# One gate-and-up product of a fused attention/SwiGLU kernel, run as two 64-row halves of TensorE

## The chip, the cores and the metric

The kernel runs on one core of a Trainium2 chip. The metric is the device time of one execution in microseconds, lower is better. Profiles are of one execution each; "span" is the time from its first to its last instruction.

## The reference

Input `x` has 2048 rows of 1024 values in bf16. `xn` is its layernorm. One branch is a local dilated attention (32 heads of 32 values, a window of 8 positions 2 apart), the other a SwiGLU MLP of inner width 3584; the result joins them:

```python
x = A_x
xn = _layernorm(x, axis=-1)
s = _A_ref(xn, A_wqkv, A_wo)              # qkv product, windowed softmax attention, product with wo
g = _silu(_B_ref(xn, B_w1, B_w3, B_w2))   # _B_ref: (silu(xn @ w1) * (xn @ w3)) @ w2
return x + s * g
```

## The kernel before

The 2048 rows are worked off in four chunks of 512 (`for c in range(NCH)`, line 592). In each chunk TensorE does, in this order:

- `qkv` (line 274): 24 groups of 8 matmuls; a group adds up the 1024 values of the contraction in 8 steps (`kt`) of 128 rows, into one PSUM tile of 128 x 512 float32. ScalarE copies each out (line 272).
- the MLP's first product, `up_block` (line 254), for 14 blocks (`FB`) of 256 columns of w1 and w3. A block has two slices of 128 columns; for each, a gate group (w1) and an up group (w3) of 8 matmuls, through `mm_group` (line 243). That makes 56 groups or 448 matmuls in a chunk. `gate_up` (line 247) follows each pair of groups: ScalarE applies silu to the gate's PSUM tile, VectorE multiplies that with the up group's PSUM tile and writes `ht`.
- the second product in two halves of the output columns (`down_half`, line 454 for its matmuls), with the attention's product with wo (line 409) in the midst of the second half.

Groups take their PSUM tiles from one pool of six (`psum_mm`). Weights come in tiles of 512 KB through SyncE's DMA queue into a pool of nine (`NS`); `take_w` hands out the next, and `load_w` issues the load of a later one once a tile has been used.

The attention's vector work, the next chunk's layernorm and the output's last steps lie in a list, `Side`. After each group or pair the program calls `side.step`, which emits as many entries as the time of that group covers, by costs written next to each entry; an entry may have a gate, an earliest time on that list's own clock. So VectorE's and ScalarE's instruction order is fixed by where these calls stand among TensorE's groups. During the first product of a chunk the list holds the query-key products (lines 299 to 314), the next chunk's statistics (line 190), its square root on ScalarE (line 216), the softmax (lines 352 to 364) with its Exp on ScalarE (line 346), and the product of probabilities and values (lines 383 and 394), which waits for a shuffle of the probabilities by DMA (`Pr<-pb`, line 372). Every engine executes its instructions in the order of the program.

Of the kernel before, what the change touches and what calls it, by code (L numbers as in the profile page):

```python
# [8 lines left out]
FP32 = mybir.dt.float32  # L9
# [36 lines left out]
def kernel(  # L46
# [11 lines left out]
    nc = tc.nc  # L58
    P = 128
    S, D, F = 2048, 1024, 3584  # L60
    Dh, W, DIL = 32, 8, 2
    KT = D // P
    CH = 512
# [3 lines left out]
    FB = FT // 2  # L67
# [4 lines left out]
    GRP = 1.727  # L72
# [13 lines left out]
    psum_mm = ctx.enter_context(tc.tile_pool(name="psum_mm", bufs=6, space=bass.MemoryType.PSUM))  # L86
# [13 lines left out]
    side = Side()  # L100

    def block(name):
        return blk.tile([P, 4096], BF16, tag="blk", name=name)
# [13 lines left out]
    def load_w(n=1, cuts=1):  # L117
        for _ in range(n):
            item = next(w_next, None)
            if item is None:  # L120
                return
            wt = wstream.tile([P, 2048], BF16, tag="w", name="w" + item[0])
            if item[0] == "q":
                _, t, a = item
                view = wt.rearrange("p (k c) -> p k c", k=2)
                src = wqkv_r[:, 2 * a:2 * a + 2, t * D:(t + 1) * D]
            elif item[0] == "2":
                _, dh, fb = item
                view = wt.rearrange("p (i n) -> p i n", n=512)
                src = w2_r[:, fb * 4:(fb + 1) * 4, dh * 512:(dh + 1) * 512]  # L130
            else:
                view = wt.rearrange("p (k f) -> p k f", k=KT)
                src = (w1_r if item[0] == "1" else w3_r)[:, :, item[1] * 256:(item[1] + 1) * 256]
            step = view.shape[1] // cuts
            for i in range(cuts):
                nc.sync.dma_start(out=view[:, i * step:(i + 1) * step, :], in_=src[:, i * step:(i + 1) * step, :])
            w_tiles.append((item, view))

    def take_w(item):
        got, wt = w_tiles.popleft()  # L140
        assert got == item, (got, item)
        return wt
# [9 lines left out]
    for st in range(1, NST):  # L152
# [7 lines left out]
    scr = const.tile([P, 1], FP32, name="scr")  # L160
# [4 lines left out]
        out=ident[:], in_=ident[:], compare_op=ALU.not_equal, fill=1.0,  # L165
# [5 lines left out]
        out=maskb[:], in_=maskb[:], compare_op=ALU.is_ge, fill=-1.0e9,  # L171
# [8 lines left out]
    def load_wo():  # L180
        was = []
        for dh in range(2):
            wa = block("wo").rearrange("p (j n) -> p j n", n=CH)
            nc.sync.dma_start(out=wa, in_=wo_r[:, :, dh * 512:(dh + 1) * 512])
            was.append(wa)
        return was
# [51 lines left out]
    def bring_one():  # L238
        if brings and brings[0][0] <= side.now:
            brings.popleft()[1]()  # L240


    def mm_group(ps, lhs, rhs):
        for kt in range(KT):
            nc.tensor.matmul(ps, lhsT=lhs(kt), rhs=rhs(kt), start=(kt == 0), stop=(kt == KT - 1))  # L245

    def gate_up(g_ps, u_ps):
        sg = sgp.tile([P, CH], BF16, tag="sg")
        nc.scalar.activation(out=sg[:], in_=g_ps[:], func=ACTF.Silu)  # L249
        ht = hp.tile([P, CH], BF16, tag="ht")  # L250
        nc.vector.tensor_mul(ht[:], sg[:], u_ps[:])  # L251
        return ht

    def up_block(c, xnT, fb):
        hts = []
        w1t, w3t = take_w(("1", fb)), take_w(("3", fb))
        for i in range(2):
            pss = []
            for wt in (w1t, w3t):
                ps = psum_mm.tile([P, CH], FP32, tag="mm", name=f"gu{c}_{fb}_{len(pss)}")  # L260
                mm_group(ps[:], lambda kt: wt[:, kt, i * P:(i + 1) * P], lambda kt: xnT[:, kt, :])
                pss.append(ps)
            if i == 1:
                load_w(2)
            hts.append(gate_up(*pss))
            side.step(2 * GRP, 0.7)
        bring_one()
        return hts
# [5 lines left out]
    def qkv(c, xnT, ts):  # L274
        for t in ts:
            w = take_q(t)
            if t == 1 and c > 0:
                nc.gpsimd.tensor_copy(out=kT[:, :, 0:HALO], in_=kT[:, :, CH:CH + HALO])
            if t == 2 and c > 0:
                nc.gpsimd.tensor_copy(out=vT[:, :, 0:HALO], in_=vT[:, :, CH:CH + HALO])  # L280
            for j in range(NJ):
                ps = psum_mm.tile([P, CH], FP32, tag="mm", name="ps_qkv")
                mm_group(ps[:], lambda kt: w(kt, j), lambda kt: xnT[:, kt, :])
                if j == NJ - 1:
                    load_w(4)
                proj_out(t, j, ps)
                side.step(GRP)
            if t == 1:
                qk_side(c)
# [125 lines left out]
    def wo_proj(pieces, was):  # L415
        side.flush()
        oT = att["oT"]
        s_sb = block("s_sb").rearrange("p (st d) -> p st d", st=NST)
        for dh, st in pieces:
            ps = wo_piece(oT, was, st, dh * CH, CH)  # L420
            nc.scalar.copy(out=s_sb[:, st, dh * CH:(dh + 1) * CH], in_=ps[:])  # L421
            side.step(GRP)
        return s_sb
# [14 lines left out]
    def finish_half(c, dh, gts, s_sb, xres, queue):  # L438
        def one(st):
            finish(c, st, dh * 512, 512, gts[st][:], s_sb[:, st, dh * 512:(dh + 1) * 512], xres, queue)  # L440
        for st in range(NST):
            side.add(1.38, lambda st=st: one(st))

    def down_half(c, dh, hts, at):
        accs = [psum_mm.tile([P, 512], FP32, tag="mm", name=f"acc{c}_{dh}_{st}") for st in range(NST)]
        gts = []
        for fb in range(7):
            w2t = take_w(("2", dh, fb))
            order = [(i, st) for i in range(4) for st in range(NST)]
            if fb in (0, 6):  # L450
                order = [(i, st) for st in range(NST) for i in range(4)]
            for n, (i, st) in enumerate(order):
                f = fb * 4 + i
                nc.tensor.matmul(  # L454
                    accs[st][:], lhsT=hts[f][:, st * P:(st + 1) * P], rhs=w2t[:, i, :],
                    start=(f == 0), stop=(f == FT - 1),
                )
                if n == 7:
                    side.step(GRP)
            load_w()  # L460
            if fb == 6:
                gts = [silu_acc(accs[st][:]) for st in range(NST)]
            side.step(GRP)
            at(fb)
        return gts

    def load_xres(c):
        xres = block("xres").rearrange("p (st d) -> p st d", st=NST)
        nc.sync.dma_start(out=xres, in_=x_flat[c * CH:(c + 1) * CH, :].rearrange("(st p) d -> p st d", p=P))
        return xres  # L470
# [18 lines left out]
    xnT = xnT_pool.tile([P, KT, CH], BF16, tag="xnT")  # L489
# [30 lines left out]
    def copy_in(tp, st, ks, eng):  # L520
# [29 lines left out]
        out=junk[:], in_=x0[2][:], func=ACTF.Square, bias=nm[:], scale=1.0 / 32.0, accum_out=mv0[2][:, 1:2],  # L550
# [40 lines left out]

    for c in range(NCH):
        qkv(c, xnT, (1, 2) if c == 0 else (0, 1, 2))
        was, hts = None, []
        for fb in range(FB):
            hts += up_block(c, xnT, fb)
            if fb == 10:
                was = load_wo()
        while brings:
            brings.popleft()[1]()  # L600
        res = {}

        def early(fb, c=c, res=res):
            if fb == 1:
                res["x"] = load_xres(c)

        gts = down_half(c, 0, hts, early)
        xres = res["x"]
        every = [(dh, st) for dh in range(2) for st in range(NST)]
        if c + 1 < NCH:  # L610
            state = {}

            def mid(fb):
                if fb == WO_AT - 1:
                    state["s"] = wo_proj(every, was)
                    finish_half(c, 0, gts, state["s"], xres, nc.gpsimd)

            gts1 = down_half(c, 1, hts, mid)
            side.flush()
            finish_half(c, 1, gts1, state["s"], xres, nc.gpsimd)  # L620
            xnT = att["x"]
        else:
            s_sb = wo_proj(every[:-1], was)
            finish_half(c, 0, gts, s_sb, xres, nc.gpsimd)
            side.flush()
            last_half(c, hts, s_sb, xres, was)
# [30 lines left out]
```

## Time and profile before

| | before |
|---|---|
| median of 3 runs | 819.64 us (818.79 to 819.96) |
| the profiled execution | 818.27 us |
| its span | 816.5 us |
| TensorE busy | 809.6 us (99%), 3820 matmuls |
| VectorE busy | 464.8 us (57%) |
| ScalarE busy | 191.5 us (23%) |
| granted TensorE clock | 1.00 |
| chunk 1: qkv | 211.21 to 252.65 us, 192 matmuls |
| chunk 1: first product | 252.65 to 349.34 us, 448 matmuls |
| chunk 1: second product, first part | from 349.34 us |

In the first product of chunk 1 (252.65 to 349.34 us) TensorE is busy throughout, VectorE for 70.1 us, ScalarE for 23.5 us, and the DMA engines are busy for a share of 0.93. Matmuls overlap in the records (each is shown from its start to a modelled end), so the pace of a stream of them is the distance of their starts, not the length of one.

### The profile page before, as it was taken

What the parts mean: (1) busy time and instruction counts of PE and PEld (TensorE: products, weight loads), DVE (VectorE), ACT (ScalarE), POOL (GpSimd) and SP (SyncE); (2) the same over time, 40 slices, a digit from 0 to 9 for tenths busy, and PEclk for the clock granted to TensorE, in tenths of its full rate; (3) what the DMA queues carried; (4) which work ended last, traced back from release to release, by engine and by line L of the source; (5) the groups of instructions that cost most, each with busy time, mean ns of one, the idle gap of its engine ahead of it and who ended that gap; (6) DMA issues with size and microseconds to landing.
All of it is one profiled execution on the core that took longest, in us unless ns stands there. A gap on an engine that the chain in (4) does not pass through costs nothing.

```text
span 816.5 us, 9525 instructions
## 1 busy us (share of the span) xinstructions
PE 809.6 (99%) x3820; PEld 406.2 (50%) x3820; DVE 464.8 (57%) x472; ACT 191.5 (23%) x310; POOL 92.4 (11%) x172
## 2 busy tenths in 40 slices
PE   8999999999999999999999999999999999999997
PEld 6654444444565444444466444444446644444443
DVE  4099574942229765692224968479311694759432
ACT  4331331012332132101133213310223321311120
POOL 0000312001100223000110031400001004130010
PEclk9999999999999999999999999999999999999999
DMA  8476999742366799965245789996424378687500
GB/s 283 136 197 202 212 182 298 242 155 78 104 192 170 221 197 214 296 207 154 78 132 152 190 221 197 210 291 206 142 90 155 104 206 204 165 220 240 177 33 20
DMA packets 190925, 146.39 MB, mean 179 GB/s; under 512 B 19360, under 2 KB 171680, under 8 KB 190880
## 3 DMA queue, kind: packets, MB, share of 16 engines
q1 hardware_dynamic: 185440, 133.71, 59.1%
q0 software_dynamic: 5440, 12.07, 6.4%
q8 instruction: 30, 0.49, 0.3%
q14 instruction: 15, 0.12, 0.1%
HBM read 130.02 MB, written 4.19 MB: 164 GB/s over the span
## 4 chain that ended last, share of the span: by engine, by line
PE 91%; DVE 4%; DMA 2%; issue 1%; ACT 1%; POOL 0%; SPq 0%; DVEq 0%; ACTq 0%
PE gu L245 40%; PE acc L454 20%; PE ps_qkv L245 19%; PE ps_wo L409 7%; PE acc L477 3%; DMA Pr<-pb 2%; PE ps_qkv L563 1%; DVE pv L383 1%; DVE ht L251 1%; DVE stats L190 1%; POOL Pr L372 0%; DMA x<-in_A_x_dram 0%; ACT L249 0%; DVE oT L394 0%; DVE pv L394 0%
## 5 line engine op out<-in xcount | busy, mean ns | idle before, releaser
L245 PE MATMUL gu<-xnT_next,w 128*128 128x512 bf16 x1344 | 290.6, 379 | 0.0
L245 PEld LDWEIGHTS <-w 128*128 128x128 bf16 x1792 | 175.3, 98 | 211.2
L454 PE MATMUL acc<-w,ht 128*128 128x512 bf16 x784 | 170.5, 379 | 0.1
L245 PEld LDWEIGHTS <-wq 128*128 128x128 bf16 x720 | 103.3, 143 | 52.1
L249 ACT ACTIVATE sg<-gu 128x512 bf16<-128x512 f32 x112 | 65.9, 597 | 261.8 <-PE gu L245 242.7
L251 DVE TENSOR_TENSOR ht<-sg,gu 128x512 bf16<-128x512 bf16 x112 | 75.8, 681 | 88.5 <-PE gu L245 70.0
L299 DVE TENSOR_TENSOR prod<-qT,kT 128x4096 bf16<-128x4096 bf16 x32 | 73.1, 2285 | 92.6 <-ACT kT L272 92.6
L245 PE MATMUL ps_qkv<-xnT_next,wq 128*128 128x512 bf16 x576 | 124.8, 379 | 0.0
L454 PEld LDWEIGHTS <-ht 128*128 128x128 bf16 x784 | 76.6, 98 | 92.9 <-issue 0.4
L245 PE MATMUL gu<-xnT,w 128*128 128x512 bf16 x448 | 96.9, 379 | 0.0
L434 DVE TENSOR_TENSOR gt<-gt,s_sb 128x512 f32<-128x512 f32 x31 | 21.4, 690 | 125.2 <-ACT gt L428 67.7
L330 POOL DMA_DIRECT2D L<-E x64 | 37.2, 588 | 273.5 <-DVE E L314 265.6
L383 DVE TENSOR_TENSOR pv<-Pr,vT 128x4096 bf16<-128x4096 bf16 x28 | 63.3, 2283 | 0.0
L310 DVE TENSOR_TENSOR prod<-prod 128x2048 bf16<-128x2048 bf16 x64 | 61.2, 956 | 1.4
L409 PE MATMUL ps_wo<-wo,oT 128*128 128x512 bf16 (+2 forms) x264 | 56.1, 373 | 0.0
L428 ACT ACTIVATE gt<-acc 128x512 f32<-128x512 f32 x32 | 19.1, 597 | 148.8 <-PE acc L454 127.0
L436 POOL DMA_DIRECT2D out_dram<-o_t x28 | 15.4, 549 | 310.5 <-DVE o_t L435 310.5
L372 POOL DMA_DIRECT2D Pr<-pb x64 | 36.8, 582 | 108.7 <-DVE pb L364 99.9
L409 PEld LDWEIGHTS <-oT 128*128 128x128 bf16 x264 | 25.6, 98 | 30.0
L394 DVE TENSOR_TENSOR oT<-oT,pv 128x4096 bf16<-128x4096 bf16 x16 | 36.6, 2287 | 0.2
L421 ACT CAST s_sb<-ps_wo 128x512 bf16<-128x512 f32 x31 | 18.2, 586 | 66.4 <-PE ps_wo L409 66.4
L245 PE MATMUL ps_qkv<-xnT,wq 128*128 128x512 bf16 x144 | 31.2, 379 | 0.0
(64 smaller groups left out, 312.2 us busy)
## 6 DMA issues: line engine op xcount, KB each, us to landing
w<-in_B_w_dram SPq DMA_DIRECT2D x168, 512.0 KB, 5.2
wq<-in_A_wqkv_dram SPq DMA_DIRECT2D x44, 512.0 KB, 3.8
wo<-in_A_wo_dram SPq DMA_DIRECT2D x8, 1024.0 KB, 10.0
L<-E POOLq DMA_DIRECT2D x64, 64.0 KB, 6.1
Pr<-pb POOLq DMA_DIRECT2D x64, 64.0 KB, 5.1
xres<-in_A_x_dram SPq DMA_DIRECT2D x4, 1024.0 KB, 6.2
out_dram<-o_t POOLq DMA_DIRECT2D x28, 128.0 KB, 2.0
x_t<-in_A_x_dram SPq DMA_DIRECT2D x12, 256.0 KB, 6.6
```

What stands on the lines that cost most here:

```text
L245: nc.tensor.matmul(ps, lhsT=lhs(kt), rhs=rhs(kt), start=(kt == 0), stop=(kt == KT - 1))
L249: nc.scalar.activation(out=sg[:], in_=g_ps[:], func=ACTF.Silu)
L251: nc.vector.tensor_mul(ht[:], sg[:], u_ps[:])
L299: nc.vector.tensor_mul(prod, qT[:], kT[:, :, o:o + CH])
L310: nc.vector.tensor_add(prod[:, 0:n, :], prod[:, 0:n, :], prod[:, n:2 * n, :])
L330: nc.gpsimd.dma_start(out=L4[sq * NH:(sq + 1) * NH, r, :, :], in_=E_r[r, :, :, sq * P:(sq + 1) * P],)
L372: nc.gpsimd.dma_start(out=Pr_r[r, :, :, sq * P:(sq + 1) * P], in_=pb[sq * NH:(sq + 1) * NH, :, :],)
L383: nc.vector.tensor_mul(dst, Pr[:, w, :].unsqueeze(1).to_broadcast([P, NJ, CH]), vT[:, :, o:o + CH])
L394: nc.vector.tensor_add(a, a, b)
L409: nc.tensor.matmul(ps[:, 0:w], lhsT=oT[:, j, st * P:(st + 1) * P], rhs=was[dh][:, j, n0:n0 + w], start=(j == 0), stop=(j == NJ - 1),)
L454: nc.tensor.matmul(accs[st][:], lhsT=hts[f][:, st * P:(st + 1) * P], rhs=w2t[:, i, :], start=(f == 0), stop=(f == FT - 1),)
L477: nc.tensor.matmul(acc[:], lhsT=hts[f][:, st * P:(st + 1) * P], rhs=w2ts[f // 4][:, f % 4, :], start=(f == 0), stop=(f == FT - 1),)
```

## The change

Chunks 0, 2 and 3 stay as they are. In chunk 1, `up_all` takes the place of the 14 calls of `up_block`. Each matmul on 128 rows of the contraction becomes two on 64 rows, one on partitions 0 to 63 (`h` = 0, a lower half) and one on partitions 64 to 127 (`h` = 1, an upper half); both add to the group's PSUM tile. The program runs over 448 + 15 steps (`LAG` = KT + 7 = 15). Step s issues the lower half of matmul s and the upper half of matmul s - 15, which belongs to the group before or to the one before that. After the last lower half of a group, ScalarE copies one column of its PSUM tile to a scratch column, so that the upper halves that go on adding to that tile are ordered behind it. `gate_up`, `side.step`, `load_w` and `bring_one` are called for the same pairs and blocks as before, once the last upper half of a pair has been issued. The load of wo, after block 10, is now called through `wo_at` in both forms.

```diff
+    LAG = KT + 7
+
+    def up_all(c, xnT, at):
+        hts, pss, tiles = [], [], {}
+
+        def half(g, kt, h):
+            blk_n, k = divmod(g, 4)
+            i, wt = k // 2, tiles[blk_n][k % 2]
+            rows = slice(h * 64, (h + 1) * 64)
+            nc.tensor.matmul(
+                pss[g][:], lhsT=wt[rows, kt, i * P:(i + 1) * P], rhs=xnT[rows, kt, :],
+                start=(kt == 0 and h == 0), stop=(kt == KT - 1 and h == 1), skip_group_check=True,
+            )
+            if h == 0 and kt == KT - 1:
+                nc.scalar.copy(out=scr[:], in_=pss[g][:, 0:1])
+
+        total = 4 * FB * KT
+        for s in range(total + LAG):
+            if s < total:
+                g, kt = divmod(s, KT)
+                if kt == 0:
+                    if g % 4 == 0:
+                        tiles[g // 4] = (take_w(("1", g // 4)), take_w(("3", g // 4)))
+                    pss.append(psum_mm.tile([P, CH], FP32, tag="mm", name=f"gu{c}_{g}"))
+                half(g, kt, 0)
+            if s >= LAG:
+                g, kt = divmod(s - LAG, KT)
+                half(g, kt, 1)
+                if kt == KT - 1 and g % 2 == 1:
+                    if g % 4 == 3:
+                        load_w(2)
+                        del tiles[g // 4]
+                    hts.append(gate_up(pss[g - 1], pss[g]))
+                    side.step(2 * GRP, 0.7)
+                    if g % 4 == 3:
+                        bring_one()
+                        at(g // 4)
+        return hts
...
     for c in range(NCH):
         qkv(c, xnT, (1, 2) if c == 0 else (0, 1, 2))
-        was, hts = None, []
-        for fb in range(FB):
-            hts += up_block(c, xnT, fb)
+        res = {}
+
+        def wo_at(fb, res=res):
             if fb == 10:
-                was = load_wo()
+                res["wo"] = load_wo()
+
+        if c == 1:
+            hts = up_all(c, xnT, wo_at)
+        else:
+            hts = []
+            for fb in range(FB):
+                hts += up_block(c, xnT, fb)
+                wo_at(fb)
+        was = res["wo"]
```

More of the change, by code (lines that the diff above doesn't have):

```diff
@@ L593 @@
         qkv(c, xnT, (1, 2) if c == 0 else (0, 1, 2))
-        was, hts = None, []
-        for fb in range(FB):
-            hts += up_block(c, xnT, fb)
+        res = {}
+        def wo_at(fb, res=res):
             if fb == 10:
-                was = load_wo()
+                res["wo"] = load_wo()
[7 more added lines that the diff above has]
+        was = res["wo"]
         while brings:
             brings.popleft()[1]()
-        res = {}
         def early(fb, c=c, res=res):
```

## The prediction

> **What bounds the kernel now.** I read the page's busy times first, then the chain that ended last, then the groups by form of TensorE and its weight loads, and last the timelines of ScalarE and VectorE in chunk 1's first product.
>
> ```profile
> PE 809.6 (99%) x3820; PEld 406.2 (50%) x3820; DVE 464.8 (57%) x472; ACT 191.5 (23%) x310; POOL 92.4 (11%) x172
> ```
>
> The chain in order of time (start, length, what, count):
>
> ```profile
> 12.50 0.45 PE tp L517 x8
> ...
> 14.71 6.56 PE ps_qkv L563 x60
> ...
> 252.65 96.69 PE gu L245 x448
> 349.34 34.53 PE acc L454 x160
> ```
>
> The stage to be changed is 448 matmuls in 96.69 us, 215.8 ns each, with no gap, and the next stage follows at once. Nothing but TensorE's own pace and new waits of TensorE can move the end; the other engines matter only where they make it wait. Two more paces stand here: 56 ns for a 128-column matmul (0.45/8), 109 ns for a 256-column one (6.56/60). A straight line through 128 and 512 columns gives 0.416 ns a column and 2.6 ns fixed.
>
> Groups by form, TensorE and its loads (last columns: busy us, mean ns, idle us):
>
> ```profile
> L245 PE MATMUL gu<-xnT_next,w 128*128 128x512 bf16 x1344 | 290.6, 379 | 0.0
> L563 PE MATMUL ps_qkv<-xnT,wq 128*128 128x256 bf16 x96 | 11.0, 273 | 0.5 <-DVE xnT L521 0.5
> L245 PEld LDWEIGHTS <-w 128*128 128x128 bf16 x1792 | 175.3, 98 | 211.2
> L563 PEld LDWEIGHTS <-wq 128*128 128x128 bf16 x96 | 10.5, 144 | 0.6 <-issue 0.6
> ```
>
> A load recorded at 144 ns disappears behind matmuls that follow each other every 109 ns: on the whole array, loads are hidden. A matmul takes 379 ns from start to end, so 163 ns of it is drain behind the next one.
>
> ScalarE's timeline (start, length, what):
>
> ```profile
> 292.40 0.60 ACT L249 ACTIVATE sg<-gu 128x512 bf16<-128x512 f32 x1 [2.86 <-PE gu L245]
> 293.01 1.28 ACT L216 ACT_TABLE_LOAD   x1
> 297.69 0.30 ACT L216 ACTIVATE rstd<-mv,eps_t 128x4 f32<-128x4 f32 x1 [3.39 <-DVE mv L213]
> 298.00 1.28 ACT L249 ACT_TABLE_LOAD   x1
> 299.30 1.09 ACT L249 ACTIVATE sg<-gu 128x512 bf16<-128x512 f32 x2
> 302.82 0.60 ACT L249 ACTIVATE sg<-gu 128x512 bf16<-128x512 f32 x1 [2.43 <-PE gu L245]
> 303.43 1.28 ACT L346 ACT_TABLE_LOAD   x1
> 310.50 1.06 ACT L346 ACTIVATE z<-z 128x1024 f32<-128x1024 f32 x1 [5.78 <-DVE z L359]
> ```
>
> and VectorE's:
>
> ```profile
> 290.74 0.69 DVE L251 TENSOR_TENSOR ht<-sg,gu 128x512 bf16<-128x512 bf16 x1 [2.77 <-PE gu L245]
> ...
> 295.57 0.64 DVE L251 TENSOR_TENSOR ht<-sg,gu 128x512 bf16<-128x512 bf16 x1
> ...
> 299.93 0.69 DVE L251 TENSOR_TENSOR ht<-sg,gu 128x512 bf16<-128x512 bf16 x1 [2.28 <-ACT sg L249]
> ...
> 304.96 0.68 DVE L251 TENSOR_TENSOR ht<-sg,gu 128x512 bf16<-128x512 bf16 x1
> ...
> 308.64 0.68 DVE L251 TENSOR_TENSOR ht<-sg,gu 128x512 bf16<-128x512 bf16 x1
> ```
>
> Twice ScalarE stands still, in program order, for VectorE: at the Sqrt of the next layernorm (nothing else until 297.99) and at the softmax's Exp (until 311.56). TensorE doesn't notice now, since only the release of PSUM tiles hangs on ScalarE, and six tiles give room. The five VectorE lines are the products of gate pairs 10, 11, 12, 13 and 14 (a pair is gate and up of one 128-column slice, 28 in the stage).
>
> **The change, part by part.**
>
> *The halves.* 448 matmuls on 128 rows become 896 on 64, written as 463 steps: 448 with a lower half of one group, 448 with an upper half of a group 15 steps behind, 433 with both. If the halves of a step truly run together, a step costs what a matmul of the same columns costs: 215.8 ns. No row of the trace shows two halves together, so the bounds are wide: below, 213.2 ns (the 2.6 ns fixed part of one matmul hidden; 448 of them make a gain of 1.2 us); above, 431.7 ns, one after the other (+96.7 us). Instructions are no bound: a step has two loads and two matmuls, and the transposes ran a load and a matmul every 56 ns, so 112 ns of 216. I take 215.8, the row of the same column count, because nothing that the trace shows is fuller than before. The Trainium skill (TensorE: Matmul & The Clock Gate, "Part 3: Packing small matmuls") has matmuls on different row groups start about 4 ns apart and then run together, which by itself would leave my sum as it is; no run here shows it yet.
>
> *The lag.* 15 steps have only a lower half and 15 only an upper one: 463 steps against 448 is 15 x 215.8 ns = 3.24 us, all on the path.
>
> *Changes between whole array and halves.* Two. Bounds: nothing, or a drain and a load in the open each, 163 + 98 ns. I take the upper one, 0.5 us: halves and whole rows can't share the array as two whole matmuls do.
>
> *The one-column copy and its wait.* After the last lower half of each group ScalarE copies one column of its PSUM tile, so the first upper half must wait for ScalarE's read. 56 copies at 0.20 us (the 128x1 ScalarE rows have 203 ns) are nothing to an engine with 23.5 of 96.7 us busy there. But ScalarE works in order, and a copy has only 8 steps = 1.73 us from its issue to the upper half that waits for it; behind that half the whole TensorE queue stands. In the plain course silu, copy and copy fit within a pair's 3.45 us. At the two standstills they don't. Let E be the end of pair 11's last step. Pair 11's silu is issued there, then Sqrt, and one step later the copy of group 25, whose upper half is due at E + 1.73.
> - Sqrt: before, it ended 7.25 us after pair 10's product began (290.74 to 297.99: three statistics, product, the fourth). VectorE idles ahead of that product, so it starts 0.27 us after pair 10's end, as now, which is at E - 3.45. Sqrt ends at E + 4.07, the copy at E + 4.27; stall 2.5 us.
> - Exp: before, pair 12's product began 1.94 us after Sqrt's end (table, silu). Now two copies lie ahead of the table load: 2.34, so E + 6.41. From there to Exp's end VectorE ran without a gap, 11.63 us (299.93 to 311.56), which gives E + 18.04; the product of pair 14, the last in it, is ready before its turn. The copy of group 31 ends at E + 18.27. It is due 1.73 us after pair 14: E + 3 x 3.45 + 2.54 + 1.73 = E + 14.63. Stall 3.6 us.
>
> Copies don't bring table loads of their own: the casts of line 272 stand next to silu without one. Together 6.1 us. Bounds: nothing if the copy were not waited for, 9 us if each wait of the profile is felt in full (3.39 + 5.78).
>
> *VectorE and PSUM.* The product now comes 15 steps later after a tile is taken, so an up tile, if tiles go round in order, is wanted again 25 steps = 5.4 us after its end instead of 41 = 8.8. Before, products were up to 8.2 us late near 343 us, because VectorE had sat 4.86 us for the probabilities' DMA. That DMA hangs on the Exp chain, which moves by about 4.4 us while TensorE moves by 9.3 there; the wait goes, and products then run at most 3.4 us late. No stall, so 0; but if the allocation reuses an up tile one pair sooner (2.2 us), the late products cost up to about 4 us.
>
> *Weights.* A block's two tiles are freed 15 steps = 3.2 us later on SP's queue. Nine tiles minus four in use leave five loaded ahead, two are needed per 6.9 us, and a load lands in 5.5 us: nothing. Cover gone, the wait would be under 3 us.
>
> Sum: 3.24 + 0.5 + 2.5 + 3.6 = **9.8 us**. The profiled execution took 818.27 us with a span of 816.5; it would become 828.1. The median shown is 1.4 us above it, so 819.64 + 9.8 = 829.4 us.
>
> **The rivals.**
>
> 1. *Weight loads in the open.* The load for a half waits until that half's rows have finished their matmul. The pair then takes up to 215.8 + 98 = 314 ns: 448 x 98 = 43.9 us, the lag 15 x 314 = 4.7, and with longer steps the copies are due later, leaving about 1 us of stalls: some +49, 868 us. Against it: whole-array loads hide wholly, on the very rows at work. For it: no load of half the rows is in the trace. The Trainium skill (same page and part, "What overlaps and what doesn't") says that a load overlaps with running matmuls only where row groups differ; this trace, with 98 ns loads inside a 216 ns pace on the same rows, contradicts that for the whole array.
> 2. *The change doesn't do what it says:* the halves run one after the other. 896 x 215.8 = 193.4 us instead of 96.7; the lag then costs nothing (the count stays 896), copies have twice the time and stalls vanish: +97, 917 us. Nothing in the trace excludes it.
> 3. *The other side:* a half, with half the rows to pass, takes less than a whole matmul's pace, and the pairs gain more than the rest costs. It decides from 9.8/448 = 22 ns a pair, that is at 194 ns; at 180 ns it would give 819.6 + 9.8 - 16.0 = 813 us. Against it: 56, 109 and 216 ns at 128, 256 and 512 columns show a pace set by columns, and columns stay 512.
>
> **How the numbers follow.** Together at 216 ns: 0.74. Own range: 823 (lag only, stalls not felt) to 838 (PSUM +4, and 10 ns a pair, +4.5). Loads in the open: 0.10. One after the other: 0.12. The other side: 0.04. The range reaches from 823 to the end of rival 1, 868, leaving out rivals 2 and 3, 0.16. About 0.2% (1.6 us) is what a measurement can tell from no change: faster 0.03, same 0.02 (rival 3 near its point, or a forecast without lag and stalls), slower 0.95.
>
> **What would show it.** Starts of lower halves 216 ns apart, each with an upper half a few ns from it; the stage 106 us long from first to last half; two gaps on TensorE, about 2.5 and 3.6 us, ended by ScalarE's copy behind Sqrt and behind Exp; no wait of VectorE for the probabilities' DMA; the stages around unchanged. The forecast is wrong if lower halves stand 300 or 430 ns apart, if gaps come at many groups (PSUM or the copies in plain course), or if the clock granted falls after a gap.

## The result, and the profile after

The change made the kernel slower: 831.11 us median (830.71 to 832.48, 4 runs) against 819.42 us (818.79 to 819.96), ratio 1.0143, 95% interval 1.0131 to 1.0155. The profiled execution took 830.71 us with a span of 828.9 us.

The page after, engine line and the groups of the new line 265 (last columns: busy us, mean ns, idle us and what ended it):

```profile
PE 811.8 (98%) x4203; PEld 410.8 (50%) x4268; DVE 465.0 (56%) x472; ACT 197.9 (24%) x366; POOL 92.0 (11%) x172
...
L265 PE MATMUL gu<-xnT_next,w 64*128 64x512 bf16 x896 | 101.0, 376 | 7.0 <-ACT scr L270 5.3
...
L265 PEld LDWEIGHTS <-w 64*128 64x128 bf16 x896 | 48.0, 94 | 60.0 <-issue 9.0
```

896 half matmuls fill 101.0 us, 113 ns each, where a whole one took 216 ns: two run beside each other. The line also names where TensorE now stands idle: behind `scr`, the one-column copy. TensorE's timeline of the kernel after shows the four places (start, length, what, count, idle time before and what ended it; three excerpts):

```profile
302.17 10.54 PE L265 MATMUL gu<-xnT_next,w 64*128 64x512 bf16 x96 [2.06 <-ACT scr L270]
315.95 2.33 PE L265 MATMUL gu<-xnT_next,w 64*128 64x512 bf16 x20 [3.25 <-ACT scr L270]
...
347.75 3.63 PE L265 MATMUL gu<-xnT_next,w 64*128 64x512 bf16 x32 [0.34 <-DVE ht L251]
352.76 1.47 PE L265 MATMUL gu<-xnT_next,w 64*128 64x512 bf16 x12 [1.37 <-DVE ht L251]
```

The idle time of the view is counted from the modelled end of the matmul before; between the starts, less the usual distance, the stream of upper halves loses 3.07, 3.43, 0.51 and 1.54 us. Of the first, 0.63 us only undo a lead that this stream had over the program's order (see the last section), so the schedule loses 2.44 us there. ScalarE's timeline of the kernel after shows the copies that the first two wait for:

```profile
296.80 0.60 ACT L249 ACTIVATE sg<-gu 128x512 bf16<-128x512 f32 x1
297.42 1.28 ACT L216 ACT_TABLE_LOAD   x1
301.77 0.30 ACT L216 ACTIVATE rstd<-mv,eps_t 128x4 f32<-128x4 f32 x1 [3.07 <-DVE mv L213]
301.98 0.33 ACT L270 COPY scr<-gu 128x1 f32<-128x1 f32 x2
...
310.02 1.28 ACT L387 ACT_TABLE_LOAD   x1
314.80 1.06 ACT L387 ACTIVATE z<-z 128x1024 f32<-128x1024 f32 x1 [3.50 <-DVE z L400]
315.76 0.33 ACT L270 COPY scr<-gu 128x1 f32<-128x1 f32 x2
```

Sqrt and Exp wait for VectorE; the copy follows each at once, and TensorE 0.04 us or so after the first copy. VectorE's timeline of the kernel after carries the other two gaps:

```profile
338.67 0.69 DVE L251 TENSOR_TENSOR ht<-sg,gu 128x512 bf16<-128x512 bf16 x1 [2.77 <-PE gu L265]
342.61 2.29 DVE L424 TENSOR_TENSOR oT<-Pr,vT 128x4096 bf16<-128x4096 bf16 x1 [3.25 <-DMA Pr<-pb]
344.82 2.29 DVE L424 TENSOR_TENSOR pv<-Pr,vT 128x4096 bf16<-128x4096 bf16 x1
347.02 0.68 DVE L251 TENSOR_TENSOR ht<-sg,gu 128x512 bf16<-128x512 bf16 x1
...
352.02 0.68 DVE L251 TENSOR_TENSOR ht<-sg,gu 128x512 bf16<-128x512 bf16 x1
```

VectorE still waits 3.25 us for the probabilities' DMA; the products at 347.02 and 352.02 end just ahead of TensorE's restarts at 347.75 and 352.76, which are the first matmuls of groups that want these products' up tiles again.

From the last whole matmul of chunk 1's qkv (start 253.00, so its turn ends at 253.22) to the first of the second product (361.28) the stage took 108.07 us instead of the 96.69 before, 11.38 more. The stages around are nearly as they were: 0.7 us more in the first 53 us of the profiled execution, and 0.3 us more behind the stage.

### The profile page after: what moved, and what is told of

Its sections match the earlier page's. It is cut to its first block, busy times and chain, and to the rows that moved or that the text cites. A ratio compares the mean times of both kernels' runs of the same rounds, so it can differ in the third digit from the quotient of the medians.

```text
span 828.9 us, 10439 instructions
## 1 busy us (share of the span) xinstructions
PE 811.8 (98%) x4203; PEld 410.8 (50%) x4268; DVE 465.0 (56%) x472; ACT 197.9 (24%) x366; POOL 92.0 (11%) x172
## 4 chain that ended last, share of the span: by engine, by line
PE 85%; DVE 7%; DMA 4%; issue 2%; POOL 1%; ACT 1%; DVEq 0%; ACTq 0%
PE gu L245 28%; PE acc L495 20%; PE ps_qkv L245 19%; PE gu L265 7%; PE ps_wo L450 7%; DMA Pr<-pb 3%; PE acc L518 3%; DVE pv L424 1%; PE ps_qkv L604 1%; DVE stats L190 1%; DVE ht L251 1%; POOL Pr L413 1%; PE warm_ps L535 1%; DVE oT L435 1%; ACT L249 0%
## 5 line engine op out<-in xcount | busy, mean ns | idle before, releaser
L245 PEld LDWEIGHTS <-w 128*128 128x128 bf16 x1344 | 131.6, 98 | 158.4
L245 PE MATMUL gu<-xnT_next,w 128*128 128x512 bf16 x878 | 192.8, 379 | 0.9
L265 PE MATMUL gu<-xnT_next,w 64*128 64x512 bf16 x896 | 101.0, 376 | 7.0 <-ACT scr L270 5.3
L265 PEld LDWEIGHTS <-w 64*128 64x128 bf16 x896 | 48.0, 94 | 60.0 <-issue 9.0
```

The source lines that it names most:

```text
L265: nc.tensor.matmul(pss[g][:], lhsT=wt[rows, kt, i * P:(i + 1) * P], rhs=xnT[rows, kt, :], start=(kt == 0 and h == 0), stop=(kt == KT - 1 a ...
```

## Experiments

Each is compared with the kernel before on the same chip. Taking the copy away outright wasn't tried: lower and upper halves would then add to one PSUM tile with nothing to order them. So the runs take away what makes the copy late, or move it.

**Sqrt and Exp one gate pair later (e2_late).** In `ln_side` (the first line stands at the end of `stat`) and `softmax_side`, for chunk 1 alone:

```diff
+            mark[1] = side.now + 1.0 if c == 2 else 0.0
...
-        side.add(0.0, root)
+        side.add(0.0, root, lambda: mark[1])
...
+        def sub():
+            nc.vector.tensor_sub(z[:], z[:], mx[:].unsqueeze(1).to_broadcast([P, W, P]))
+            mark[1] = side.now + 1.0 if c == 1 else 0.0
...
-        side.add(0.0, expo)
+        side.add(0.0, expo, lambda: mark[1])
```

> The changed kernel, with the Sqrt of the next layernorm and the Exp of the softmax emitted one gate pair later in chunk 1 (a gate on each entry of the list), so that VectorE has finished what they read before ScalarE comes to them. Theory A (the two large gaps of TensorE, 2.4 and 3.4 us, are upper halves waiting for a one-column copy that stands behind Sqrt or Exp on ScalarE): gaps of at most 0.3 us each are left, and TensorE comes earlier to the late products of the probabilities stage, so that their gaps shrink too; 831.1 - 5.5 to - 7.5, that is 823.5 to 825.5 us. Rival B (the gaps come from VectorE's lateness through the release of PSUM tiles, and the copy is only the last name in the record): they stay in sum, 829 to 831 us.

Measured: 822.68 us, ratio 1.0040 (1.0028 to 1.0053). ScalarE's timeline of this kernel, and TensorE's over the stage:

```profile
301.47 0.30 ACT L217 ACTIVATE rstd<-mv,eps_t 128x4 f32<-128x4 f32 x1
301.68 0.14 ACT L271 COPY scr<-gu 128x1 f32<-128x1 f32 x1
...
315.61 1.06 ACT L392 ACTIVATE z<-z 128x1024 f32<-128x1024 f32 x1 [0.34 <-DVE z L388]
316.58 0.35 ACT L271 COPY scr<-gu 128x1 f32<-128x1 f32 x2
```

```profile
252.62 100.57 PE L266 MATMUL gu<-xnT_next,w 64*128 64x512 bf16 x896
```

Sqrt no longer waits, Exp waits 0.34 us, and of TensorE's four gaps one of 0.25 us is left. 8.4 us of the 11.7 are gone, a little more than expected, because the two late PSUM gaps vanished too; why these did is argued only: the probabilities stage now starts later among the pairs, so fewer products stand behind its long multiplications (the first of these starts 10.9 us before TensorE's stage ends, at 342.25 us; in the kernel after it was 18.7 us, from 342.61). Theory A stands, rival B falls. What is left, 3.3 us by the medians and 3.9 us in the profiled stage, is mostly the lag (3.24).

**The same move in the kernel before (e6_before_late),** the same edit on the kernel before.

> The kernel before, with the same later emission of Sqrt and Exp in chunk 1 as in e2_late and nothing else. Theory A: in the kernel before TensorE doesn't wait for ScalarE, so this moves nothing: 819.4 us, within 0.2%. Rival: the later emission is itself worth something (better order of VectorE's work), and part of the 8.4 us that e2_late took back comes from that: 815 to 818 us.

Measured: 818.98 us, ratio 1.0002 (0.9993 to 1.0010). The later emission is worth nothing by itself that can be told from the scatter; what e2_late took back was the new wait.

**A lag of 23 steps (e3_lag23).**

```diff
-    LAG = KT + 7
+    LAG = KT + 15
```

> The changed kernel with a lag of 23 steps instead of 15. Theory A together with the PSUM account (an up tile is wanted again 17 steps after its end instead of 25): lag +1.73 us, the gap at Sqrt down from 2.4 to about 0.7, the one at Exp from 3.4 to about 2.9 because the late Sqrt no longer holds TensorE back, and waits for PSUM tiles up from 2.1 to about 5 or more; in all 833 to 835 us. Rival C (PSUM room plays no part, only the copies' due time counts): 831.1 + 1.7 - 1.7 - 1.7 = 829.4 us.

Measured: 832.39 us, ratio 1.0161 (1.0146 to 1.0176), 0.6 us below what A gave and 3 us above C. TensorE's timeline of this kernel:

```profile
303.71 7.46 PE L265 MATMUL gu<-xnT_next,w 64*128 64x512 bf16 x65 [0.34 <-ACT scr L270]
311.56 3.61 PE L265 MATMUL gu<-xnT_next,w 64*128 64x512 bf16 x31 [0.40 <-DVE ht L251]
317.51 28.39 PE L265 MATMUL gu<-xnT_next,w 64*128 64x512 bf16 x257 [2.34 <-ACT scr L270]
347.44 3.63 PE L265 MATMUL gu<-xnT_next,w 64*128 64x512 bf16 x32 [1.54 <-DVE ht L251]
352.44 1.90 PE L265 MATMUL gu<-xnT_next,w 64*128 64x512 bf16 x16 [1.37 <-DVE ht L251]
```

The copy at Sqrt is nearly in time, the one at Exp still isn't, and waits for products (`ht`) come up in new places: a longer lag buys time for the copy and pays with PSUM room.

**Eight PSUM tiles going round (e4_psum8).**

```diff
-                    pss.append(psum_mm.tile([P, CH], FP32, tag="mm", name=f"gu{c}_{g}"))
+                    pool, tag = (psum_aux, "aux") if g % 4 == 3 else (psum_mm, "mm")
+                    pss.append(pool.tile([P, CH], FP32, tag=tag, name=f"gu{c}_{g}"))
```

> The changed kernel, with every fourth group of chunk 1's first product in a tile of the second PSUM pool (two tiles, idle in this stage), so that eight tiles go round instead of six. If the two smaller gaps near the end of the stage (0.6 and 1.5 us) are waits for an up tile whose product is late, they vanish and the two large ones stay: 829.0 us. If they are something else (a weight tile, a record that is missing): 831 us.

Measured: 829.56 us, ratio 1.0126 (1.0108 to 1.0143). The two small gaps are gone, the two large ones stay (2.06 and 3.17 us idle in the view, 2.06 and 3.25 after). They were waits for up tiles (the PSUM tiles of up groups, which a late product still reads). This execution also showed something else. Busy times in stretches of this kernel (PE, PEld, DVE, ACT, POOL, then the granted clock, DMA share, GB/s):

```profile
299.40:301.80 2.40, 0.39 (x2) 0.00 (x0) 1.98 (x5) 0.34 (x2) 0.00 (x0) 0.96 1.18 287
301.80:305.30 3.50, 3.46 (x18) 1.46 (x19) 0.00 (x0) 2.04 (x3) 0.00 (x0) 0.54 0.17 45
305.30:308.00 2.70, 2.70 (x28) 1.37 (x26) 2.58 (x6) 0.82 (x3) 0.00 (x0) 1.00 0.00 0
```

After the gap at Sqrt the granted clock is 0.54 for 3.5 us, and steps stand 427 ns apart instead of 216: 1.6 us lost on top of the gap.

**Transposes ahead of the shuffle (e5_early_t).**

```diff
-                    if g % 4 == 3:
-                        bring_one()
+                    bring_one()
+                    if g % 4 == 3:
                         at(g // 4)
```

> The changed kernel, with the DMA transposes of the next chunk's rows issued up to once a gate pair instead of once a block, so that all four are issued before the probabilities' shuffle. Theory D (the shuffle took 19.7 us instead of 15.9 because two transposes now fell into it): it takes 16 to 17 us, the products are less late, the two smaller gaps shrink by 1.5 to 2: 829.1 to 829.6 us. Rival (the weight loads alone make it slow): it stays at 19 to 20 us, 831 us.

Measured: 829.61 us, ratio 1.0123 (1.0107 to 1.0139). SyncE's timeline of the kernel before, of the kernel after and of this one, around the shuffle (318.3 to 334.2 us before, 322.8 to 342.5 after, 323.3 to 339.3 here):

```profile
315.30 3.18 SPq L226 DMA_TRANSPOSE xnT_next<-x_t  x1
...
322.20 2.03 SPq L226 DMA_TRANSPOSE xnT_next<-x_t  x1
```

```profile
325.24 3.72 SPq L226 DMA_TRANSPOSE xnT_next<-x_t  x1
329.95 2.10 SPq L136 DMA_DIRECT2D w<-in_B_w_dram  x2
332.14 4.55 SPq L226 DMA_TRANSPOSE xnT_next<-x_t  x1
```

```profile
318.91 3.49 SPq L226 DMA_TRANSPOSE xnT_next<-x_t  x2
324.92 14.18 SPq L136 DMA_DIRECT2D w<-in_B_w_dram  x5
```

With no transpose issued during it, the shuffle took 16.1 us instead of 19.7, and TensorE had no gap in the probabilities stage. Weight loads went on beside it, so the rival falls, and theory D's forecast came true. Its reason, that more transposes than before fell into the shuffle, is not shown. These are the DMA packets during the shuffle of the kernel before, of the kernel after and of this one:

```profile
DMA packets 6011, 4.21 MB, mean 265 GB/s; under 512 B 2448, under 2 KB 5755, under 8 KB 6011
```

```profile
DMA packets 6424, 3.84 MB, mean 195 GB/s; under 512 B 2432, under 2 KB 6167, under 8 KB 6423
```

```profile
DMA packets 4756, 3.31 MB, mean 205 GB/s; under 512 B 915, under 2 KB 4499, under 8 KB 4755
```

Of the packets under 512 bytes, 2048 are the transposes' (256 bytes each) both before and after: two transposes' data lay beside the shuffle before as well, since the one issued at 315.30 us moved its data after 318.5. What differs is their place. After, the second transpose moved its data from 337.3 to 342.0 us, over the last three transfers of the shuffle, which took 8.3 to 8.6 us from issue to landing; before, the last three took 4.1 to 5.3 us, here 3.5 to 5.8. Nor is the shuffle's length steady: the four of the kernel before took 17.7, 15.9, 18.0 and 14.4 us. How much of the 3.8 us is the place of the transposes and how much is scatter stays open. Here too, 3.4 us after the gap at Exp ran at a clock of 0.53.

**The copy on VectorE (e9_copy_dve).**

```diff
+    vscr = const.tile([P, 1], FP32, name="vscr")
...
-                nc.scalar.copy(out=scr[:], in_=pss[g][:, 0:1])
+                nc.vector.tensor_copy(out=vscr[:], in_=pss[g][:, 0:1])
```

> The changed kernel with the one-column copy on VectorE instead of ScalarE. Theory A (TensorE waits for whatever stands ahead of the copy on its engine): the two gaps at Sqrt and Exp give way to gaps of 1 to 4 us at some twenty groups, wherever VectorE's queue is 1.7 us or more behind, in sum 40 to 50 us more than the kernel before: 860 to 875 us, some more if the clock falls after the gaps. Rival B (the gaps come from the release of PSUM tiles by late products): little changes, 829 to 833 us.

Measured: 882.53 us, ratio 1.0775 (1.0755 to 1.0795): theory A's way, but 7.5 us above its range (two runs). The instructions on the copy's tile in this kernel:

```profile
L271 DVE COPY vscr<-gu x56: 103/154/160, 257.7 to 409.2; 128x1 f32<-128x1 f32 x56
...
who waited for it (us, times):
  POOL L L372: 83.5, 1
  PE gu L266: 40.4, 19
```

19 groups wait 40.4 us for copies of 0.15 us. The waits are in sum what was expected. What the range had no price for was the clock, which fell to about half after eight of the longer gaps, for 37.5 us in all; the mean over the execution was 0.978. Rival B is excluded.

**Halves without a lag (e8_quad),** with e2_late's and e4_psum8's edits:

```diff
+            for n, (lo, hi) in enumerate(((A, B), (C, D), (B, A), (D, C))):
...
+                for kt in range(KT):
+                    half(lo, kt, 0, n < 2)
+                    half(hi, kt, 1, n < 2)
...
+                    hts.append(gate_up(pss[hi], pss[lo]))
```

The last line is reached in the two rounds that end a pair (`n` of 2 and 3).

> Halves in chunk 1 without a lag: a block's four groups A to D run as lower A beside upper B, lower C beside upper D, lower B beside upper A, lower D beside upper C, 8 steps each; copies and waits as in the change, Sqrt and Exp one gate pair later, every fourth tile from the second PSUM pool. If lag, copies behind Sqrt and Exp, and PSUM room are all that the change costs, what is left is two changes between whole array and halves, 0.2 us, and a wait of some tenths here or there: 819.5 to 820.3 us. Rival: halves cost something of their own in each step, or the turn from a group's lower to its upper halves does, and the time stays near e2_late's 822.7 us or above it.

Measured: 819.25 us, ratio 1.0004 (0.9995 to 1.0013). Busy times over the stage of this kernel, and TensorE's timeline:

```profile
252.69:349.79 97.10, 97.07 (x897) 45.64 (x897) 64.73 (x76) 31.90 (x90) 18.38 (x32) 1.00 0.91 222
```

```profile
252.79 97.07 PE L266 MATMUL gu<-xnT_next,w 64*128 64x512 bf16 x896
```

896 halves without an idle time of note; 97.10 us for the stage against 96.69, and 0.2 of the 0.4 is one short wait; the other 0.2 are the two changes between whole array and halves. The halves themselves cost nothing.

**That form in all four chunks (e10_quad_all),** the conditions on `c` taken out.

> e8_quad's form in all four chunks, with Sqrt and Exp a gate pair later in each. If a step of two halves costs exactly a whole matmul, the time is the kernel before's plus four times what e8_quad has, 820 to 822 us, the clock at 1.00. If each step had a cost of its own of 5 ns, 1792 of them would show 9 us: 828 us.

Measured: 821.02 us, ratio 1.0022 (1.0013 to 1.0031). Three stages took 97.10 us each, the fourth 98.01 with one wait of 1.1 in place of 0.2. A step of two halves costs a whole matmul's 215.8 ns; 5 ns more would have shown as 9 us. None of these kernels beats the kernel before.

## Why the prediction was right, and where it wasn't

It gave 829.4 us where 831.11 was measured: 9.8 us more than before against 11.7. By its terms, with the records of the profiled execution:

| term | predicted us | measured us |
|---|---|---|
| 448 steps of two halves | 0 | 0 (216 ns a step) |
| the lag, 15 steps | 3.24 | 3.24 |
| two changes between whole array and halves | 0.5 | 0.19 |
| copy behind Sqrt | 2.5 | 2.44 |
| copy behind Exp | 3.6 | 3.43 |
| waits for PSUM tiles | 0 | 2.05 |
| sum | 9.8 | 11.35 of the stage's 11.38 |

*The halves.* Starts of the stream of lower halves are 215.8 ns apart, with an upper half 20 ns after each (the prediction looked for a few ns), and e8_quad and e10_quad_all bear the price of zero out. Rival 1 is refuted: loads of half the rows, 94 ns each, lie behind matmuls of the same rows as those of the whole array did, so the Trainium skill's sentence (TensorE: Matmul & The Clock Gate, "What overlaps and what doesn't") that loads overlap only with other row groups doesn't hold here either. Rival 2 is refuted by 101.0 us of busy time for 896 halves. Rival 3's faster half doesn't exist: a half's starts are as far apart as a whole matmul's.

*The copy.* The chain statistics, Sqrt, copy, upper half was sized within 0.2 us at both places by shifting the durations of before. It could be, because VectorE ran without a gap in the rows it was taken from. The rest is shown by e2_late, e6_before_late and e9_copy_dve together: the wait belongs to the engine on which the copy stands.

*The changes of form.* The starts on either side are 312 and 309 ns apart instead of 216, so 0.10 and 0.09 us each, not the drain and a load in the open.

*The step that failed* is "that DMA hangs on the Exp chain ...; the wait goes, and products then run at most 3.4 us late". The chain did shift as said (probabilities ready 4.5 us later, at 322.79 us), but I took the shuffle's length of before, 15.9 us, as fixed, though it ranged from 14.4 to 18.0 us over the four chunks of that kernel. It took 19.7 us. VectorE waited after all, 3.25 us where it had waited 4.86 before:

```profile
334.27 2.29 DVE L383 TENSOR_TENSOR oT<-Pr,vT 128x4096 bf16<-128x4096 bf16 x1 [4.86 <-DMA Pr<-pb]
```

So the products' up tiles were wanted too soon. I had kept this cost as the upper bound (4 us) and set the value at 0; it was 2.05. That late products and too few up tiles made it is shown: e4_psum8 and e5_early_t each remove it in their own way. Why the shuffle itself became longer is shown only in part (see e5_early_t). A slip in the same passage changes no term: before, an up tile was wanted again 40 steps (8.6 us) after its end, not 41 (8.8).

A small part of the agreement is luck: the terms that were set too high (0.5 us in sum) cover a quarter of the one left at 0.

*The clock.* The prediction named a fall of the clock after a gap as a sign of being wrong. The profiled execution shows none (mean 1.000), but the three others have means of 0.995 to 0.998. In e4_psum8 one slow stretch of 3.4 us took 0.002 off the mean and cost 1.6 us. What it cost here can't be separated: the execution at 0.995 took 831.19 us, the one at 1.000 took 830.71.

## What to carry to other kernels

A read put in only to order two writers has the price of the queue in which it stands: find out what that engine waits for, in program order, between the read's issue and its use, and move the long waits or the read. When TensorE is moved against a chain of another engine, transfers tied to the one shift against transfers tied to the other, and a DMA's length of before is not a constant: here a shuffle took 14.4 to 18.0 us within one execution of the kernel before, and 19.7 us in the changed chunk. And before splitting a matmul that already streams as fast as its columns allow, ask what the split is to fill: here two halves gave exactly one whole, and all that remained was the price of the schedule.

## What the hardware showed beyond this

The section on the kernel before says that every engine executes its instructions in the order of the program. By the records, the upper halves didn't start in that order against the lower ones. The first upper half is issued after 16 lower ones, but its stream starts at 255.921 us, right after the 13th (255.913), and both streams then run at 216 ns. What waits for an upper half gained nothing by it: the last one of pair 10 starts at 293.704 us, but the semaphore that tells of its end counts at 294.729, 1.03 us later, where it is 0.39 us for a lower half (292.820 to 293.210) and about 0.4 us for both after the gap at Sqrt. So the ends were told in the program's order. The Trainium skill (TensorE: Matmul & The Clock Gate, "What overlaps and what doesn't") has matmuls start and end strictly in order; here only the ends agree. The gap at Sqrt undid the lead, so it didn't shorten the stage: after the last lower half 15 upper ones ran alone.

A pause of TensorE of 2.4 us was enough, in one execution (e4_psum8), to bring the granted clock to 0.54 for 3.5 us; pauses of 2.4 and 3.4 us in another (after) were not. The trace's own record of the clock in e4_psum8 has the fall to one half at 301.60 us, within the pause, for 3.41 us; in e9_copy_dve each of the eight slow stretches lasts 3.41 or 6.83 us. The Trainium skill (TensorE: Matmul & The Clock Gate, "What's actually happening") describes a free-running window of 3.4 us, which fits the length of the slow stretches and that the same pause may or may not bring one on; but it asks for an idle window, and here a pause shorter than that was enough.
